# A two-layer spectral and gated network on one core: the 32-point transforms as 64x64 matrix cells, two frequency groups at a time

## The chip, the cores and the metric

The kernel runs on one core of a Trainium2 chip. The metric is device time in microseconds (us) of one execution; the median of several runs counts, and less is better. The engines are named as in the profile: PE multiplies matrices (PEld is its weight loading), DVE and ACT are the vector and the scalar engine, POOL is GpSimd, SP issues most DMAs. SBUF is the on-chip memory, PSUM the accumulator memory that PE writes, with eight banks of 128 partitions by 512 float32.

## What is computed

Two layers, each a global spectral filter and a bilinear gated block, on an input of 2048 rows by 512 features in float32:

```python
x = x + irfft2(rfft2(layernorm(x)) * (w_r + 1j * w_i))     # over rows (2048) and features (512)
h = layernorm(x)
x = x + ((h @ w_gate) * (h @ w_up)) @ w_down               # 512 -> 1792 -> 512
```

Both lines are executed twice, with the same weights in both layers.

## The kernel before

The rows are split as 2048 = 64 x 32. One spectral filter is three stages. The **forward stage** (`fwd`, `fwd_rest`, line 528 on) takes 16 row tiles `t`: it folds and transforms the 512 features, then multiplies by a twiddled 64-point matrix (`times`, tile `sp`, four products with 64 rows of the array each), and ACT copies the spectrum into `E`, with 256 feature frequencies and one edge frequency (index 256).

The **middle stage** (`middle`, line 606) does the 32-point transforms, the filter and the inverse 32-point transforms. Before the change it goes over 16 groups `n` of 16 frequencies, each a tile of 128 partitions (real and imaginary part, two row halves, 32 points) by 512 elements. For one group:

1. `turn(n, False)`: DVE transposes 32x32 blocks of `E` into `T`.
2. PE multiplies by the block matrix `f2` (128x128, with four copies of a 32-point matrix and zeros between) into the PSUM bank `zp`.
3. The complex product with the filter. Eleven groups of 16: ACT copies the two halves of `zp` crosswise with a change of sign into `jz` (two instructions of 64 partitions), DVE multiplies `zp` by the filter's real part, POOL multiplies `jz` by its imaginary part, and DVE adds the two into `ys`. Five groups (`PE_ADDS`: 2, 6, 8, 10, 14): ACT copies `zp` to `jz` with one instruction, DVE and POOL multiply as before, and PE does the addition by multiplying `ys` by `g2` and `jz` by `g2j` into the same bank.
4. PE multiplies by the inverse matrix `g2` into the bank `yp`, ACT copies it back to `T`, and `turn(n, True)` transposes it on DVE into `E`.

The edge frequency is done by a small product of 32 columns (`xp`, `tx`) whose result DVE adds to group 0; group 0's first frequency takes its filter from `hp` by separate small instructions.

The filter's pieces come by SP in eight loads of 1 MB (`wq`, `wr`); two of them, pieces 6 and 7, are loaded when pieces 0 and 1 are no longer wanted. In the same stretch of the first layer POOL and ACT also split the first weights of the gated block into high and low parts (`wt` from `rg`, `wd` and `u` from `rw`).

The **inverse stage** (`inv`, line 687) multiplies rows of `E` by twiddles (`vp`), transforms the features (`yi`), and adds to `xs`, the running value. Then `build_x` (line 757) lays the normalised rows out as high and low parts (`xA`, `xS`, with the help of `sx` or `sw`), and the gated block's products (`gx`, `gy`, `gz`, `gw`, `gv`, `db`, `ex` and the like) begin. They fill most of the time.

What sets the order: every piece of work is an operation of `Plan` with an engine, a price and a due time. `Plan.order` simulates the engines, the buffers and the DMA bus with these prices, and repeats this with 163 changes of due times drawn from the seeds in `MOVES`; the instructions are then issued in the order of the last simulation. Each engine works through its own instructions strictly in that order. Due times of the middle stage are 2.1 us a group, and the stage after it is due 36 us later (line 1099). Small float32 buffers such as `jz` and `ys` share the ring `f` of ten; the PSUM banks are the rings `x`, `y`, `w` (one each), `d` (two) and `a` (three).

Of the kernel before, what the change touches and what calls it, by code (L numbers as in the profile page):

```python
# [26 lines left out]
def consts():  # L27
# [32 lines left out]
    r[64:, :, 64:] = c  # L60
    c, s = _cs(j[:, None] * j[None], 32)
    z = np.zeros((32, 32))
    bd = lambda a: np.block([[a, z], [z, a]])
    f2 = np.block([[bd(c), bd(-s)], [bd(s), bd(c)]])
    g2 = np.block([[bd(c), bd(s)], [bd(-s), bd(c)]]) / 2048
    mid = np.concatenate([f2, g2, np.concatenate([g2[64:], -g2[:64]]), np.eye(128)], 1).astype(np.float32)
# [4 lines left out]
PE_ADDS = (2, 6, 8, 10, 14), (2, 6, 8, 10, 14)  # L71
POOL_ADDS = (), ()
# [13 lines left out]
MOVES = (  # L86
# [19 lines left out]
RATE = 270.0  # L106
WARM = 2
EARLY = 0
HOLD, FAR = {"DVE": 1.0, "ACT": 1.0, "POOL": 1.0}, 15.0
CLEAR = 1.5  # L110
FREE = ("a", "f", "st", "s1", "s2", "s3")
LOOK, SLACK = 0.08, 20.0
# [21 lines left out]


class Draw:


    def __init__(self, seed):
        self.at = seed * 0x9E3779B97F4A7C15 % 2 ** 64  # L140

    def part(self):
        self.at = (self.at + 0x9E3779B97F4A7C15) % 2 ** 64
        z = self.at
        z = (z ^ z >> 30) * 0xBF58476D1CE4E5B9 % 2 ** 64
        z = (z ^ z >> 27) * 0x94D049BB133111EB % 2 ** 64
        return ((z ^ z >> 31) >> 11) * 2.0 ** -53

    def one(self, of):
        return of[int(self.part() * len(of))]  # L150

    def bell(self):
        return (self.part() + self.part() + self.part() + self.part() - 2.0) * 1.7320508


class Plan:
# [38 lines left out]
    def order(self, hop=0.12):  # L195

        ops = self.ops
        for o in reversed(ops):
            d = min([ops[s]["due"] for s in o["suc"]] + [1e9 if o["due"] is None else o["due"]])
            o["due"] = d - 1.1 * o["lag"] - hop - 0.3 * (o["e"] == "PE")  # L200
        self.kinds = [(o["e"], *(t.name for t in o["tiles"])) for o in ops]
        out, marks = self.run([], [])
        for n in MOVES:
            out, marks = self.run(out, *self.move(n, out, marks)[:1])
        return out

    def move(self, n, out, marks):


        ops, draw = self.ops, Draw(n)  # L210
        end = max(o["end"] for o in out)
        lo, span = -20.0 + draw.part() * (end + 10.0), draw.one((10.0, 20.0, 40.0, 80.0, 160.0))
        share, jit, way = draw.one((0.0, 0.25, 0.5, 1.0)), draw.one((0.0, 0.0, 2.0, 5.0)), draw.part()
        inside = [o for o in ops if lo < o["start"] < lo + span]
        if way < 0.4 and inside:
            kind, by = self.kinds[draw.one(inside)["i"]], 8.0 * draw.bell()
            for o in inside:
                if self.kinds[o["i"]] == kind:
                    o["due"] += by
        elif way < 0.7 and inside:  # L220
            for _ in range(1 + int(3.0 * draw.part())):
                draw.one(inside)["due"] += 8.0 * draw.bell()
        elif inside:
            self.latest(out, end)
            shifts = sorted(o["late"] - o["due"] for o in inside)
            shift = shifts[len(shifts) // 2]
            for o in inside:
                o["due"] += share * (o["late"] - shift - o["due"]) + jit * draw.bell()
        return [m for m in marks if m[1] < lo - 15.0], lo + span

    def latest(self, out, end):
        ops = self.ops
        nxt, two = {}, None
        for o in reversed(out):
            long = o["end"] - o["start"]
            late = end - long
            for s in o["suc"]:
                late = min(late, ops[s]["late"] - (0.0 if ops[s]["next_to"] is o else long))
            if o["e"] in nxt:
                late = min(late, nxt[o["e"]] - o["pitch"])  # L240
            if o["two"]:
                if two is not None:
                    late = min(late, two - o["pitch"])
                two = late
            for t in o["tiles"]:
                if t in self.after:
                    late = min(late, self.after[t]["late"] - long)
            nxt[o["e"]] = late
            o["late"] = late

    def run(self, best, marks, pace=None, look=LOOK, hop=0.12, slack=SLACK):

        ops = self.ops
        marks = list(marks)
        m, rings, free, bus, port, after = 0, {}, {"SP": 0.75, "AQ": 0.75, "PE": 0.9, "POOL": 0.5}, 0.75, 0.0, {}
        if marks:
            m, _, rings, free, bus, port, after = marks[-1]
        rings, free, after, out = {g: list(q) for g, q in rings.items()}, dict(free), dict(after), best[:m]
        done, mark = sum(o["e"] == "PE" for o in out), marks[-1][1] if marks else 0.0
        ready, turn = {}, {}  # L260
        for o in ops:
            o["n"], o["out"] = len(o["pre"]), False
            for t in o["tiles"]:
                t.left, t.slot, t.freed, t.due = t.users, None, 0.0, None
        for o in out:
            o["out"] = True
            for s in o["suc"]:
                ops[s]["n"] -= 1
            for t in o["tiles"]:
                t.left -= 1  # L270
                t.slot, t.freed = True, max(t.freed, o["end"])
        for o in sorted(ops, key=lambda o: (o["due"], o["i"])):
            for t in o["tiles"]:
                if t.due is None:
                    t.due = o["due"]
                    if t.slot is None:
                        turn.setdefault(t.ring, []).append(t)

        def enter(o):
            o["at"] = max([ops[p]["start" if ops[p] is o["next_to"] else "end"] for p in o["pre"]], default=0.0)  # L280
            ready.setdefault(o["e"], []).append(o)

        for o in ops:
            if not o["n"] and not o["out"]:
                enter(o)
# [961 lines left out]
```

## Time and profile before

| | us |
|---|---|
| runs: lowest, median, highest of 3 | 1091.39, 1092.04, 1097.29 |
| profiled execution: span from its first to its last instruction (the profile gives no other time for it) | 1088.8 |
| PE busy | 1073.3 (99%) |
| DVE busy | 835.3 (77%) |
| POOL busy | 728.6 (67%) |
| ACT busy | 456.7 (42%) |
| first middle stage, from DVE's first transpose to the first full-rate product of the inverse stage | 48.84 to 85.73 |
| second middle stage, likewise | 590.96 to 626.90 |

The profile names work by the tile that it writes and the tiles that it reads, `out<-in`, with buffer numbers left out: `zp<-T,midt` is a product with the matrix `midt` into `zp`. All operations are recorded at one line, so names tell them apart. A float32 product appears as two MATMUL records. PE's busy time is modelled from its pipeline, so a busy PE need not be at its peak. In the chain of work that ended last, every piece is followed back to what released it.

### The profile page before, as it was taken

To read this page: it belongs to the slowest core of one execution; us is meant where nothing else is said; L and a number is where in the kernel's file an instruction comes from. 1 tells how busy PE (TensorE), PEld (TensorE's weight loads), DVE (VectorE), ACT (ScalarE), POOL (GpSimd) and SP (SyncE) were. 2 spreads that over 40 slices of the span, in tenths; PEclk is the share of its full clock that TensorE was granted. 3 is DMA by queue.
4 is the path that set the end of the run, shared out by engine and by line. 5 is a ranking of instruction groups with operands and counts; after the bars stand their busy time and mean duration, and the time that the engine had idled before them with its cause. 6 is when DMAs were issued, how large, how long until landed. Compare 5 with 4: busy or idle time off the path is not lost.

```text
span 1088.8 us, 18587 instructions
## 1 busy us (share of the span) xinstructions
PE 1073.3 (99%) x6484; PEld 923.3 (85%) x6484; DVE 835.3 (77%) x1684; ACT 456.7 (42%) x1045; POOL 728.6 (67%) x938
## 2 busy tenths in 40 slices
PE   8999999999999999999999999999999999999998
PEld 6748988888899988888996489888889998888887
DVE  8497957777878766776797978777888876667777
ACT  6787643334442223323347776133443521222230
POOL 6486799797988665556774627566556984666680
PEclk9999999999999999999999999999999999999999
DMA  8564256574652655555354313565545256555542
GB/s 316 190 224 158 86 204 243 201 260 152 236 203 76 208 184 200 169 180 170 112 198 151 135 54 101 204 196 168 175 151 192 70 193 223 190 181 188 197 146 78
DMA packets 50445, 189.56 MB, mean 174 GB/s; under 512 B 5296, under 2 KB 19248, under 8 KB 39344
## 3 DMA queue, kind: packets, MB, share of 16 engines
q0 software_dynamic: 16128, 102.77, 28.7%
q1 hardware_dynamic: 33792, 85.01, 22.1%
q8 instruction: 52, 0.85, 0.3%
q10 hardware_dynamic: 432, 0.59, 0.1%
q14 instruction: 41, 0.34, 0.1%
HBM read 145.62 MB, written 42.73 MB: 173 GB/s over the span
## 4 chain that ended last, share of the span: by engine, by line
PE 90%; DVE 6%; DMA 2%; ACT 1%; issue 1%; POOL 0%; SPq 0%; DVEq 0%; ACTq 0%
PE gz L389 14%; PE gx L389 14%; PE db L389 7%; PE gv L389 7%; PE gw L389 7%; PE gy L389 7%; PE ex L389 5%; PE ez L389 5%; PE yi L389 3%; PE sp L389 3%; PE ey L389 3%; PE ev L389 3%; PE ew L389 3%; PE dp L389 2%; PE vp L389 2%; PE zp L389 2%
## 5 line engine op out<-in xcount | busy, mean ns | idle before, releaser
L389 PE MATMUL gx<-xA,wt 128*128 128x512 f32 (+1 forms) x852 | 180.8, 347 | 1.4 <-DVE xA L389 1.1
L389 PEld LDWEIGHTS gx<-xA,wt 128*128 128x128 f32 x852 | 136.6, 190 | 18.6 <-DVE xA L389 1.5
L389 DVE TENSOR_TENSOR q<-gy,s 128x512 f32<-128x512 f32 (+1 forms) x71 | 41.1, 578 | 79.9 <-PE gy L389 75.0
L389 DVE TENSOR_TENSOR xs<-xs,db 128x512 f32<-128x512 f32 x128 | 86.3, 683 | 18.3 <-PE db L389 18.1
L389 POOL TENSOR_TENSOR sf<-cc,sf 128x256 fp32r<-128x256 f32 x101 | 74.3, 738 | 32.9 <-ACT sf L389 32.4
L389 ACT CAST sf<-q 128x256 fp32r<-128x256 f32 x90 | 36.7, 408 | 132.6 <-DVE q L389 76.8
L389 POOL DMA_DIRECT2D wt<-gu x72 | 40.2, 558 | 76.0 <-PE gz L389 57.5
L389 PE MATMUL gz<-xS,wt 128*128 128x512 f32 (+1 forms) x426 | 90.1, 347 | 0.7 <-DVE q L389 0.7
L389 PE MATMUL gw<-xS,wt 128*128 128x512 f32 (+1 forms) x426 | 90.4, 347 | 0.0
L389 PE MATMUL gv<-xS,wt 128*128 128x512 f32 (+1 forms) x426 | 90.2, 347 | 0.0
L389 PE MATMUL db<-wd,h 128*128 128x512 f32 x336 | 90.1, 394 | 0.0
L389 PE MATMUL gy<-xS,wt 128*128 128x512 f32 (+1 forms) x426 | 89.9, 346 | 0.0
L389 PE MATMUL gz<-xA,wt 128*128 128x512 f32 (+1 forms) x426 | 89.8, 346 | 0.0
L389 POOL TENSOR_TENSOR sf<-q,sf 128x256 fp32r<-128x256 f32 x90 | 66.5, 740 | 21.3 <-ACT sf L389 19.8
L389 PEld LDWEIGHTS gz<-xA,wt 128*128 128x128 f32 x426 | 69.6, 189 | 9.9
L389 PEld LDWEIGHTS gy<-xS,wt 128*128 128x128 f32 x426 | 68.9, 189 | 9.3 <-issue 0.3
L389 PEld LDWEIGHTS gz<-xS,wt 128*128 128x128 f32 x426 | 68.5, 190 | 9.7 <-DVE q L389 1.2
L389 PEld LDWEIGHTS gw<-xS,wt 128*128 128x128 f32 x426 | 68.3, 190 | 8.7 <-DVE gz L389 0.3
L389 PEld LDWEIGHTS gv<-xS,wt 128*128 128x128 f32 x426 | 68.1, 190 | 8.1
L389 ACT CAST sf<-cc 128x256 fp32r<-128x256 f32 x101 | 41.0, 406 | 76.8 <-PE ez L389 22.6
L389 ACT COPY s<-gx 128x512 f32<-128x512 f32 (+1 forms) x71 | 35.2, 496 | 86.8 <-PE gx L389 81.0
L389 POOL TENSOR_TENSOR wt<-rg,wt 128x512 fp32r<-128x512 f32 (+1 forms) x56 | 63.7, 1154 | 8.8 <-ACT wt L389 8.7
(169 smaller groups left out, 2667.2 us busy)
## 6 DMA issues: line engine op xcount, KB each, us to landing
wt<-gu POOLq DMA_DIRECT2D x36, 1024.0 KB, 5.3
wt<-gu POOLq DMA_DIRECT2D x36, 768.0 KB, 4.7
bf<-dn POOLq DMA_DIRECT2D x20, 1024.0 KB, 5.5
bf<-dn POOLq DMA_DIRECT2D x20, 768.0 KB, 4.7
gu<-wt SPq DMA_DIRECT2D x14, 1024.0 KB, 6.6
gu<-wt SPq DMA_DIRECT2D x14, 768.0 KB, 3.5
wq<-in_wf_dram SPq DMA_DIRECT2D x10, 1024.0 KB, 6.2
rg<-in_wb_dram SPq DMA_DIRECT2D x14, 512.0 KB, 4.6
```

The source lines that it names most:

```text
L389: ins = f(*args, **kw)
```

## The change

It touches the middle stage, its constants and the order of the whole program.

The matrices shrink to 64x64 (real and imaginary part by 32 points) and stand twice, on partitions 0 to 63 and 64 to 127. Rows of the constants of the forward and the inverse stage are permuted so that a partition half holds one row half `b` (real and imaginary). The loop goes over eight pairs `m` of frequency groups. Its forward product is four cells, one for each of two groups `par` and two row halves `b`; the cell reads partitions of half `b`, and writes partitions of half `par` in bank `zp[b]`. After it a partition half is one group instead of one row half:

```diff
-            pe(0.86, lambda z=z, n=n: TE.matmul(z(), f2, T()[:, 16 * n:16 * n + 16], start=True, stop=True), [(T, n), "midt"], [zp])
+            zp = [bank("zp", tag) for tag in ("xy", "dd")[i % 2]]
+            def spec(zp=zp, m=m):
+                for par, b in ((0, 0), (1, 1), (1, 0), (0, 1)):
+                    n = 2 * m + par
+                    cell(k3(zp[b], half[par]), f2[b], T()[half[b], 16 * n:16 * n + 16], True, True)
+            pe(0.88, spec, [(T, 2 * m), (T, 2 * m + 1), "midt"], zp)
```

All additions of the complex product go to PE: for each bank one full copy by ACT, one product by the real part, one by the imaginary part, and two accumulated rounds of four cells, with `g2` and with `g2j`:

```diff
+            for b in range(2):
+                alone = (m, b) in ON_DVE_MID
+                if not alone:
+                    act(512, lambda b=b, q=q, zp=zp: A.copy(q[b](), k3(zp[b])), [zp[b]], [q[b]])
+                if (m, b) in on_pool:
+                    pool(512, lambda b=b, q=q, y=y, m=m: gtt(y[b](), q[b](), W(m, 0, b), ALU.mult), [q[b], W.key(m, 0)], [y[b]])
+                else:
+                    dve(512, lambda b=b, y=y, zp=zp, m=m: tt(y[b](), k3(zp[b]), W(m, 0, b), ALU.mult), [zp[b], W.key(m, 0)], [y[b]])
+                if alone:
+                    dve(512, lambda b=b, q=q, zp=zp, m=m: tt(q[b](), k3(zp[b]), W(m, 1, b), ALU.mult), [zp[b], W.key(m, 1)], [q[b]])
+                else:
+                    pool(512, lambda b=b, q=q, m=m: gtt(q[b](), q[b](), W(m, 1, b), ALU.mult), [q[b], W.key(m, 1)], [q[b]])
+            yp = [bank("yp", tag) for tag in ("aa", "aw")[i % 2]]
+            cells = (0, 0), (1, 1), (0, 1), (1, 0)
+            def unspec(g, z, edge, start, yp=yp, m=m):
+                for par, b in cells:
+                    cell(k3(yp[par], half[b]), g[par], z[b]()[half[par]], start, not start and m + par > 0)
+                for b in range(2 * (m == 0)):
+                    cell(yp[0]()[half[b], 0:32], g[0], ty[:, edge, b], False, not start)
+            for g, z, edge in ((g2, y, 0), (g2j, q, 1)):
+                pe(0.88 + 0.08 * (m == 0), lambda g=g, z=z, edge=edge, f=unspec: f(g, z, edge, edge == 0),
+                   [*z, *([("ty", edge, b) for b in range(2)] if m == 0 else []), *(yp if edge else ())], yp)
```

with `ON_POOL_MID = ((3, 0), (5, 0))` and `ON_DVE_MID = ((7, 0), (7, 1))`. The transposes (`turn`, two at each end of a pair) and ACT's copies of `yp` to `T` stay, 32 and 16 of them in a stage. Group 0's first frequency is written into the filter's own buffers once (`W.edge`, two small ACT copies), and the edge frequency takes one small transpose, two small cells, four small DVE products (`ty`) and two small cells in each round of pair 0. Loads have the same sizes as before, but for the matrix (96 KB and 64 KB in place of 192 KB and 64 KB).

The order of the whole program is no longer simulated: `ORDER` is a written-out list of all 4987 operations, and `Plan.order` reads it. The due times behind it have 3.3 us a pair in the middle stage and 29 us from it to the next (`MID`, in place of 36).

More of the change, by code (lines that the diff above doesn't have):

```diff
@@ L193, in op @@
         return o
[L195 to L244, printed above, removed]
-            for t in o["tiles"]:
[L246 to L285, printed above, removed]
-        while len(out) < len(ops):
-            nexts = []
-            for e, cand in sorted(ready.items(), key=lambda r: free.get(r[0], 0.0)):
-                if nexts and free.get(e, 0.0) > min(a for a, _ in nexts) + look:
-                    break
-                can = []
-                for o in cand:
-                    at = max(o["at"], free.get(e, 0.0), port if o["two"] else 0.0)
-                    if e == "SP":
-                        at = max(at, o["due"] - o["ahead"])
-                    want, early = {}, False
-                    for t in o["tiles"]:
-                        if t.slot is None:
-                            early = early or t.due > turn[t.ring][0].due + (slack if t.ring in self.FREE else 0.0)
-                            want[t.ring] = want.get(t.ring, 0) + 1
-                    if early:
-                        continue
-                    for g, n in want.items():
-                        when = sorted(t.freed for t in rings.get(g, ()) if not t.left)
-                        n -= self.RINGS.get(g, 1) - len(rings.get(g, ()))
-                        at = max(at, 1e9 if n > len(when) else when[n - 1] if n > 0 else 0.0)
-                    if at < 1e9:
-                        can.append((at, o))
-                if can:
-                    first = min(a for a, _ in can)
-                    take = min(((a, o) for a, o in can if a <= first + look), key=lambda c: (c[1]["due"], c[1]["i"]))
-                    if e in HOLD:
-                        soon = [(a, o) for a, o in can if a < take[0] + HOLD[e] * take[1]["pitch"] and o["due"] < take[1]["due"] - FAR]
-                        take = min(soon, key=lambda c: (c[1]["due"], c[1]["i"]), default=take)
-                    nexts.append(take)
-            if not nexts:
-                raise AssertionError([(o["e"], o["i"], [t.ring for t in o["tiles"]]) for c in ready.values() for o in c][:40])
-            first = min(a for a, _ in nexts)
-            if first > mark + 20.0:
-                mark = first
-                marks.append((len(out), first, {g: list(q) for g, q in rings.items()}, dict(free), bus, port, dict(after)))
-            at, o = min((c for c in nexts if c[0] <= first + look), key=lambda c: (c[1]["due"], c[1]["i"]))
-            if o["e"] == "PE":
-                assert not pace or at < pace[done]
-                done += 1
-            ready[o["e"]].remove(o)
-            for t in o["tiles"]:
-                if t.slot is None:
-                    t.slot = True
@@ L330, in run, with order @@
+    def order(self):
+        ops = [self.ops[int(ORDER[i:i + 3], 36)] for i in range(0, len(ORDER), 3)]
+        rings, done = {}, set()
+        for n, o in enumerate(ops):
+            assert o["pre"] <= done
+            done.add(o["i"])
+            for t in o["tiles"]:
+                if not t.users:
+                    continue
+                if t.left == 0:
+                    t.left = t.users
                     q = rings.setdefault(t.ring, [])
@@ L332, in run @@
                     if len(q) == self.RINGS.get(t.ring, 1):
-                        old = min((u for u in q if not u.left), key=lambda u: u.freed)
-                        after[old] = o
+                        old = min((u for u in q if not u.users), key=lambda u: u.freed)
                         q.remove(old)
@@ L337, in run @@
                     q.append(t)
-                    turn[t.ring].remove(t)
-            o["start"] = at
-            free[o["e"]] = at + o["pitch"]
-            if o["two"]:
-                port = at + o["pitch"]
-            if o["kb"]:
-                bus = max(bus, at) + o["kb"] / RATE
-                o["end"] = max(at + o["lag"], bus + 2.3)
-            else:
-                o["end"] = at + o["lag"] + hop + 0.3 * (o["e"] == "PE")
+                t.freed = n
             for t in o["tiles"]:
                 t.left -= 1
-                t.freed = max(t.freed, o["end"])
-            out.append(o)
-            for s in o["suc"]:
-                ops[s]["n"] -= 1
-                if not ops[s]["n"]:
-                    enter(ops[s])
-        self.after, self.marks = after, marks
-        return out, marks
+                if not t.left:
+                    t.users = 0
+        assert len(done) == len(self.ops)
+        return ops
 @with_exitstack
@@ L430 @@
     pe(0.86, lambda: TE.matmul(wp()[:, 0:256], warm()[:, 0:128], warm()[:, 0:256], start=True, stop=True), [warm], [(wp, 9)], due=5.5)
-    midt = cp.tile([128, 512], F32, name="midt")
-    f2, g2, g2j, ident = (midt[:, 128 * i:128 * i + 128] for i in range(4))
+    midt = cp.tile([128, 320], F32, name="midt")
+    f2, g2, g2j = ([midt[64 * r:64 * r + 64, 64 * i:64 * i + 64] for r in range(2)] for i in range(3))
+    ident = midt[:, 192:320]
     def aq(kb, fn, w, due, lag):
@@ L597, in load, with key, __call__, edge @@
             load(1024, lambda: SP.dma_start(self.at[n][2](), wf[:, n // 2, n % 2]), (), [self.at[n][0]])
-        def key(self, n, i):
-            return self.at[2 * (n // 4) + i][0]
-        def __call__(self, n, i, lo=0):
-            kw = 16 * (n % 4)
-            return self.at[2 * (n // 4) + i][2]()[:, kw + lo:kw + 16]
-    def middle(E, W, t0, adds):
+        def key(self, m, i):
+            return self.at[2 * (m // 2) + i][0]
+        def __call__(self, m, i, b):
+            at = 32 * (m % 2) + 16 * b
+            return self.at[2 * (m // 2) + i][2]()[:, at:at + 16]
+        def edge(self):
+            for i in range(2):
+                act(64, lambda i=i: A.copy(self.at[i][2]()[0:64, 0:32:16], hp[:, i, 0].rearrange("p (b g) -> p b g", b=2)),
+                    ["hp"], [self.at[i][0]])
+    def middle(E, W, t0, on_pool):
         T = temp("T", "xS", (128, 256, 32))
+        first = [(E, t, j) for t in range(15) for j in range(2)]
         def turn(n, back, due=None):
@@ L610, in turn @@
             t = lambda: T()[:, 16 * n:16 * n + 16].rearrange("p k (t j) -> p k t j", j=2)
-            es = [(E, t_, j) for t_ in range(15) for j in range(2)] + [(E, 15, j, n > 3) for j in range(2)]
             if back:
@@ L614, in turn @@
             else:
-                dve(512, lambda: V.transpose(t(), e()), es, [(T, n), (E, "b", n)], due=due)
-        def times_w(z, jz, w, p):
-            return ((lambda: A.mul(jz()[0:64], z()[64:128], -1.0)), (lambda: A.copy(jz()[64:128], z()[0:64])),
-                    (lambda: tt(p(), z(), w(0), ALU.mult)), (lambda: gtt(jz(), jz(), w(1), ALU.mult)))
-        order = [1, 2, 3, 0, *range(4, 16)]
-        for i in range(16):
-            n = order[i]
-            if n == 8:
+                dve(512, lambda: V.transpose(t(), e()), first + [(E, 15, j, n > 3) for j in range(2)], [(T, n), (E, "b", n)], due=due)
@@ new lines, in cell, with last_bin, spec @@
+        def cell(o, w, z, start, stop):
+            TE.matmul(o, w, z, start=start, stop=stop, skip_group_check=True)
+        k3 = lambda o, rows=slice(0, 128): o()[rows].rearrange("p (k g) -> p k g", g=32)
+        half = [slice(0, 64), slice(64, 128)]
+        def last_bin(due):
+            dve(100, lambda: V.transpose(tx.rearrange("p (t j) -> p t j", j=2), E()[:, :, 256]),
+                first + [(E, 15, j, True) for j in range(2)], ["tx"], due=due)
+            xp = [bank("xp", "aw"[b]) for b in range(2)]
+            def spec():
+                for b in range(2):
+                    cell(xp[b]()[0:64, 0:32], f2[b], tx[half[b]], True, True)
+            pe(0.15, spec, ["tx", "midt"], xp)
+            for b in range(2):
+                dve(40, lambda b=b: tt(ty[:, 0, b], xp[b]()[0:64, 0:32], hp[:, 0, 1, 32 * b:32 * b + 32], ALU.mult),
+                    [xp[b], "hp"], [("ty", 0, b)])
+                dve(40, lambda b=b: tt(ty[:, 1, b], xp[b]()[0:64, 0:32], hp[:, 1, 1, 32 * b:32 * b + 32], ALU.mult),
+                    [xp[b], "hp"], [("ty", 1, b)])
@@ L642, in middle @@
-            zp = bank("zp", "xydwd"[i % 5])
-            z = lambda zp=zp: zp().rearrange("p (k g) -> p k g", g=32)
-            pe(0.86, lambda z=z, n=n: TE.matmul(z(), f2, T()[:, 16 * n:16 * n + 16], start=True, stop=True), [(T, n), "midt"], [zp])
-            q = temp("jz", "f", (128, 16, 32))
-            y = temp("ys", "f", (128, 16, 32))
-            where = adds[n]
-            fs = times_w(z, q, lambda i, n=n: W(n, i), y if where != "DVE" else z)
-            if where == "PE":
-                act(512, lambda z=z, q=q: A.copy(q(), z()), [zp], [(q, 0), (q, 1)])
-            else:
-                act(512, fs[0], [zp], [(q, 0)], more=0.11)
-                act(512, fs[1], [zp], [(q, 1)], more=0.11)
@@ L674, in middle @@
-            yp = bank("yp", "a")
-            ms = [y, q] if where == "PE" else [y]
-            def unspec(yp=yp, ms=ms):
-                y3 = yp().rearrange("p (k g) -> p k g", g=32)
-                for j, m in enumerate(ms):
-                    TE.matmul(y3, g2j if j else g2, m(), start=j == 0, stop=j == len(ms) - 1)
-            pe(0.86 * len(ms), unspec, [y, (q, 0), (q, 1)], [yp])
-            act(512, lambda yp=yp, n=n: A.copy(T()[:, 16 * n:16 * n + 16], yp().rearrange("p (k g) -> p k g", g=32)),
-                [yp], [(T, n)], more=0.07)
@@ L685, in middle @@
-            turn(n, True, due)
+            due = t0 + 8 + MSTEP * i
+            for par in range(2):
+                turn(2 * m + par, False)
+            if m == 0:
+                last_bin(due)
+            zp = [bank("zp", tag) for tag in ("xy", "dd")[i % 2]]
[3 more added lines that the diff above has]
+                    cell(k3(zp[b], half[par]), f2[b], T()[half[b], 16 * n:16 * n + 16], True, True)
@@ new lines, in middle @@
+            pe(0.88, spec, [(T, 2 * m), (T, 2 * m + 1), "midt"], zp)
+            q = [temp("jz", "f", (128, 16, 32)) for _ in range(2)]
+            y = [temp("ys", "f", (128, 16, 32)) for _ in range(2)]
+            for b in range(2):
+                alone = (m, b) in ON_DVE_MID
[9 more added lines that the diff above has]
+                    pool(512, lambda b=b, q=q, m=m: gtt(q[b](), q[b](), W(m, 1, b), ALU.mult), [q[b], W.key(m, 1)], [q[b]])
@@ L687, in inv @@
+            for par in range(2):
+                n = 2 * m + par
+                act(512, lambda yp=yp, n=n, par=par: A.copy(T()[:, 16 * n:16 * n + 16], k3(yp[par])), [yp[par]], [(T, n)], more=0.07)
+                turn(n, True, due)
     def inv(t, nm, E, di, mode, tags, due=None, on_act=False, early=None):
@@ L1075, in down @@
         add(gz, R[1], 0, at(7) + 0.7)
-    ADDS = [{n: "PE" if n in PE_ADDS[i] else "POOL" if n in POOL_ADDS[i] else "DVE" for n in range(16)} for i in range(2)]
     dcs = {}
@@ L1097 @@
         W.load(3)
[L1098 to L1099 removed]
+        middle(E, W, t0, ON_POOL_MID)
+        t0 += MID
         X = temp("xA", "xA", (128, 3, 2, 2, 512), F32R), temp("xS", "xS", (128, 4, 2, 2, 512), F32R)
```

239 lines of the change are left out of this document (169 added, 70 removed), and 19 rows, old and new, of the table MOVES.

## The prediction

> **What bounds the kernel now.** I read the page first.
>
> ```profile
> span 1088.8 us, 18587 instructions
> PE 1073.3 (99%) x6484; PEld 923.3 (85%) x6484; DVE 835.3 (77%) x1684; ACT 456.7 (42%) x1045; POOL 728.6 (67%) x938
> DVE  8497957777878766776797978777888876667777
> PE 90%; DVE 6%; DMA 2%; ACT 1%; issue 1%; POOL 0%; SPq 0%; DVEq 0%; ACTq 0%
> ```
>
> Over the whole span PE is the bound. But DVE's slices have 9s in two places, and 6% of the chain is DVE. A table of windows, cut at the two middle stages, shows whose stages these are (columns: length, then busy time of PE, PEld, DVE, ACT and POOL, clock, DMA share, GB/s):
>
> ```profile
> 0.00:48.80 48.80, 45.53 (x326) 35.34 (x326) 29.39 (x105) 34.13 (x87) 26.55 (x40) 1.00 0.66 235
> 48.80:85.70 36.90, 34.71 (x88) 15.42 (x88) 36.80 (x64) 29.09 (x55) 30.92 (x29) 1.00 0.60 227
> 85.70:103.80 18.10, 18.06 (x118) 16.77 (x119) 12.38 (x40) 14.12 (x36) 8.45 (x12) 1.00 0.57 200
> 103.80:590.90 487.10, 484.42 (x2948) 426.00 (x2946) 365.41 (x734) 193.57 (x443) 357.36 (x439) 1.00 0.53 181
> 590.90:626.90 36.00, 34.22 (x89) 15.61 (x89) 35.85 (x64) 25.54 (x48) 20.86 (x19) 1.00 0.36 124
> 626.90:1075.00 448.10, 447.06 (x2872) 406.87 (x2873) 345.51 (x659) 159.05 (x378) 283.41 (x400) 1.00 0.48 160
> 1075.00:1088.80 13.80, 9.27 (x48) 7.31 (x46) 9.96 (x19) 1.22 (x3) 1.02 (x2) 1.00 0.41 153
> ```
>
> In the second and fifth row DVE is busy 36.80 of 36.90 us and 35.85 of 36.00. The stage cannot be shorter than DVE's list of work. PE is busy some 34 us beside it, so DVE's list alone could give 2 us at most; the change cuts PE's work there too, which is costed below. The chain has the same ends (start, length, what):
>
> ```profile
> 48.84 0.72 DVE T L389
> 80.91 4.78 DVE E L389 x8
> 85.73 2.64 PE vp L389 x20
> ...
> 590.96 0.72 DVE T L389
> 622.67 4.19 DVE E L389 x7
> 626.90 1.70 PE vp L389 x12
> ```
>
> Each stage starts with DVE's first transpose and ends when its last one lets the inverse stage's `vp` go. So what leaves DVE's list shortens the span, until another engine or the filling and draining of the pipeline takes over.
>
> **The change, part by part. DVE.** The groups of DVE's instructions in the first stage (the second has the same counts):
>
> ```profile
> L389 DVE STREAM_TRANSPOSE T<-E 128x512 f32<-128x512 f32 x16 | 10.3, 680 | 6.0 <-ACT E L389 6.0
> L389 DVE STREAM_TRANSPOSE E<-T 128x512 f32<-128x512 f32 x16 | 10.3, 679 | 0.0
> L389 DVE TENSOR_TENSOR ys<-zp,jz 128x512 f32<-128x512 f32 x11 | 7.3, 660 | 0.0
> L389 DVE TENSOR_TENSOR zp<-zp,wq 128x512 f32<-128x512 f32 (+1 forms) x9 | 5.9, 673 | 0.0
> L389 DVE TENSOR_TENSOR ys<-zp,wq 128x512 f32<-128x512 f32 x3 | 2.0, 668 | 0.0
> L389 DVE TENSOR_TENSOR ys<-ys,tx 128x32 f32<-128x32 f32 x1 | 1.2, 1155 | 0.0
> L389 DVE TENSOR_TENSOR zp<-zp,hp 128x32 f32<-128x32 f32 x1 | 0.2, 199 | 0.0
> ```
>
> Two more rows hold four products with `wr`. That makes 32 transposes, 16 products and 11 additions, 59 large instructions. One lasts 0.67 us, but they overlap: seven transposes in 4.19 us are 0.599 each, and 59 x 0.599 = 35.3 of the 36.9 us. Small ones fill the rest; `ys<-ys,tx` alone is 1.2 us.
>
> Afterwards there are 32 transposes, 14 products with the real part (two of 16 go to POOL) and two with the imaginary part (`ON_DVE_MID`): 48 x 0.599 = 28.8 us. The 11 additions are gone. The small ones become one transpose and four products, costed at 0.1 us apart (the 0.2 us of `zp<-zp,hp` overlaps as the large ones do): 0.5 us. Sum 29.3 us of DVE work in each stage.
>
> To it comes time that DVE cannot fill. At the start it has 16 transposes to go on with. At the end the last pair's second round (0.86 us, below) and ACT's copy must pass before its transpose:
>
> ```profile
> 625.23 0.58 ACT L389 COPY T<-yp 128x512 f32<-128x512 f32 x1 [0.27 <-PE yp L389]
> ```
>
> 0.86 + 0.27 + 0.58 is 1.7, with the steps between engines some 1.8 us if no other transpose is left, and nothing if three are held back, as the seven and eight in a row above are now. I take 0.5, near the lower end since transposes are held back now, and keep 0 to 1.8. So 29.8 us (29.3 to 31.1).
>
> **PE.** Whether it stays below this depends on the cells. Nothing in the trace has 64x64 cells; the nearest rows are products on half the array's rows, beside full ones:
>
> ```profile
> 45.59 2.87 PE L389 MATMUL sp<-us,tw 64*128 64x257 f32 x24
> 45.58 2.47 PEld L389 LDWEIGHTS sp<-us,tw 64*128 64x128 f32 x24
> 49.61 4.56 PE L389 MATMUL zp<-T,midt 128*128 128x512 f32 x10 [1.16 <-DVE T L389]
> 69.63 1.88 PE L389 MATMUL zp<-T,midt 128*128 128x512 f32 x4
> ...
> L389 PEld LDWEIGHTS zp<-T,midt 128*128 128x128 f32 x64 | 11.6, 189 | 18.9 <-issue 10.0 <-DVE T L389 6.8 <-DVE ys L389 0.8
> ```
>
> A full product of 512 columns is two records, 0.86 us apart from the next (four records in 1.88, their last one ending 0.16 late; ten in 4.56). The run of `sp` is three times four products of 256 columns, which by that pace would take 3 x 1.72 = 5.2 us one after another; it took 2.87. So products on the two row halves do run at once, and two of 512 columns cost 0.95 where the ideal is 0.86. Loads of their weights come every 0.10 us (2.47/24), so they too overlap.
>
> If all four cells of a round run at once, a round costs 0.86, or 0.95 with the loss of `sp`. There are three rounds a pair, 24 a stage: 20.6 to 22.8 us, below DVE's 29.3. If only the row halves overlap, a round is two such steps, 1.72 to 1.90. I take the lower, because cells on different column halves have as little in common as cells on different row halves, and keep the higher for a rival.
>
> The full-height rows say something of weight loading: ten records with ten loads of 0.19 us between them stand 0.43 apart, so the loads are hidden behind products on the same rows. [...]
>
> **POOL and ACT.** POOL multiplies 14 imaginary parts and two real ones, 16 large instructions as now; two small ones go.
>
> ```profile
> L389 POOL TENSOR_TENSOR jz<-jz,wr 128x512 f32<-128x512 f32 x8 | 10.1, 1269 | 2.8 <-ACT jz L389 2.8
> L389 POOL TENSOR_TENSOR wt<-rg,wt 128x512 fp32r<-128x512 f32 (+1 forms) x5 | 5.8, 1164 | 2.6 <-ACT wt L389 2.6
> 103.78 1.54 POOL L389 TENSOR_TENSOR sx<-sx 128x256 f32<-128x256 f32 x2 [7.82 <-ACT sx L389]
> ```
>
> 16 x 1.27 = 20.3 us is below 29.3. In the first stage POOL has weights to split besides, and its 30.92 us would fill a stage of 29.8. That work need not end there: after it POOL waits 7.8 us for `sx`, just before 103.8. A stage shorter by 7.1 uses that wait up almost wholly; with the idle inside the stage it still fits. The second stage has 20.86 us of POOL work, no such limit. ACT loses the crosswise halves: 14 copies and 16 to `T` at 0.58 are 17.4 us, where it is busy 25 to 29 now. DMA sizes are the same, and pieces 6 and 7 of the filter are asked for after the same groups, so they come no later against the loop.
>
> **The rest of the program** gets another order. In the windows outside the middle stages, start and end, PE is idle 0.04 + 2.68 + 1.04 = 3.8 us, so a better order has under 4 us to win there and some 3 at the start (48.80 less 45.53). A worse one can lose; the nearest row is POOL's 7.8 us wait, one stall of that length. With no reason for a sign I take 0.
>
> **The sum.** First stage 36.9 - 29.8 = 7.1 us, second 36.0 - 29.8 = 6.2 us, together 13.3. The span goes from 1088.8 to 1075.5. The median of the runs, 1092.0, lies 3.2 above the span (start and end outside it), which I carry over: 1078.7, so **1079 us**. With the bounds of the tail the same sum is 1077.7 to 1081.3.
>
> **The rivals.**
>
> *Row halves only (slower).* Two cells on the same rows but different columns do not run at once. Then a stage is PE's: 24 rounds of 1.72 to 1.90 are 41.3 to 45.6 us, with 1.2 us of transposes ahead and 2.1 behind (ACT's copy and two transposes) 44.6 to 48.9; two stages lose 16 to 25 us: 1108 to 1117. It decides from a round of 29.3/24 = 1.22 us on. [...] Against it: row halves do run so, and the loads hide.
>
> *POOL takes DVE's place in the first stage.* If its weight work stays ahead of the products, or the products come in bunches, `sx` is late. At worst the first stage's 7.1 us are lost: 1086; half of it gives 1082. For it: 30.92 us of work in a stage of 29.8. Against it: its wait of 7.8.
>
> *The order is better or worse elsewhere.* Better by the 4 to 7 us of idle PE time: 1072 to 1075. Worse by one stall of 7.8: 1087.
>
> **How the numbers follow.** Forecast 0.56 (own range 1076 to 1083), POOL in the first stage 0.14 (1082 to 1086), better order 0.12 (1071 to 1076), worse order 0.09 (1083 to 1092, split evenly at the bound below), row halves only 0.09. About 0.5%, or 5.5 us, is what a measurement of this kernel can tell from no change: faster is below 1086.5. So faster is 0.56 + 0.14 + 0.12 + 0.04 = 0.86, the same 0.05, slower 0.09. The range takes the forecast, POOL and most of both orders: 1071 to 1087.
>
> **What would show it.** In the profile after: middle stages of some 30 us, with DVE busy nearly throughout and no `ys<-zp,jz` rows; 48 large DVE instructions in each; PE busy some 21 to 25 us in them, and each round of eight `zp` or `yp` records within 0.86 to 0.95 us; ACT's busy time in both down by some 14 us together; POOL's wait for `sx` nearly gone. Rounds of 1.7 us or more, with DVE idle for `zp` or `yp`, would show the slower rival. A first middle stage of 30 us followed by a longer way to the first `gx` would show POOL's. A stage above 32 us with DVE idle inside would mean that filling and draining cost more than 1.8, which makes this sum wrong.

## The result, and the profile after

The median after is 1077.56 us (1076.85 to 1077.94, 4 runs) against 1091.72 us before (1089.9 to 1097.29, 4 runs). The ratio is 0.9858, with a 95% interval of 0.9828 to 0.9887: 1.4% faster. The profiled execution took 1076.85 us, with a span of 1075.1, so 1.75 us lie outside the span.

From the page of the kernel after:

```profile
span 1075.1 us, 19053 instructions
PE 1056.2 (98%) x6740; PEld 917.3 (85%) x6740; DVE 823.0 (77%) x1662; ACT 438.4 (41%) x1019; POOL 730.6 (68%) x934
PE 92%; DVE 5%; ACT 1%; issue 1%; POOL 0%; DMA 0%; DVEq 0%; POOLq 0%; ACTq 0%
```

The windows of the kernel after, cut at its own middle stages (columns as in the prediction's table):

```profile
49.34:79.66 30.32, 26.74 (x221) 14.07 (x221) 29.35 (x53) 18.86 (x38) 24.71 (x23) 0.94 0.53 196
79.66:97.20 17.54, 16.59 (x108) 15.34 (x109) 11.14 (x38) 13.94 (x35) 15.77 (x18) 1.00 0.68 241
97.20:584.28 487.08, 484.70 (x2954) 427.02 (x2952) 367.74 (x738) 194.73 (x449) 358.96 (x440) 1.00 0.54 184
584.28:613.75 29.47, 26.73 (x216) 11.31 (x217) 29.35 (x53) 16.25 (x32) 20.39 (x17) 1.00 0.43 151
```

The first row and the last are the two stages, 30.32 and 29.47 us, with DVE busy 29.35 us in both. Before they were 36.89 (48.84 to 85.73) and 35.94 (590.96 to 626.90). So 6.57 + 6.47 = 13.04 of the 13.7 us between the spans come out of these two stages; the remaining 0.7 us is the sum of small differences elsewhere (0.5 longer ahead of the first stage, 0.6 shorter between the stages and 0.6 behind the second). In the clock column, the first row's 0.94 is new; below it gets a part of its own.

The chain of the kernel after has the stages' ends where they were, at DVE's first transpose and at its last (the x8 and x7 rows are the transposes in a row that end a stage):

```profile
74.84 4.78 DVE E L353 x8
79.66 2.18 PE vp L353 x16
...
584.28 0.72 DVE T L353
609.52 4.19 DVE E L353 x7
613.75 1.70 PE vp L353 x12
```

DVE's groups of the kernel after in the second stage:

```profile
L353 DVE STREAM_TRANSPOSE T<-E 128x512 f32<-128x512 f32 x16 | 10.3, 679 | 5.9 <-ACT E L353 5.9
L353 DVE STREAM_TRANSPOSE E<-T 128x512 f32<-128x512 f32 x16 | 10.2, 683 | 0.0
L353 DVE TENSOR_TENSOR ys<-zp,wq 128x512 f32<-128x512 f32 x11 | 7.1, 662 | 0.1
L353 DVE TENSOR_TENSOR ys<-zp,wr 128x512 f32<-128x512 f32 x3 | 1.9, 673 | 0.0
L353 DVE TENSOR_TENSOR jz<-zp,wq 128x512 f32<-128x512 f32 x2 | 1.3, 666 | 0.0
L353 DVE TENSOR_TENSOR ty<-xp,hp 64x32 f32<-64x32 f32 x4 | 0.5, 168 | 0.0
```

48 large instructions, no `ys<-zp,jz`. And PE's rounds of four cells, from the timeline of PE of the kernel after (start, length with the tail of the last record, what):

```profile
595.81 1.09 PE L353 MATMUL zp<-T,midt 64*64 64x512 f32 x8
596.72 1.04 PE L353 MATMUL yp<-jz,midt 64*64 64x512 f32 x8
597.57 1.04 PE L353 MATMUL yp<-ys,midt 64*64 64x512 f32 x8
598.43 1.44 PE L353 MATMUL zp<-T,midt 64*64 64x512 f32 x6
```

The second, third and fourth start 0.85 and 0.86 us apart: four cells of 512 columns take as long as one product on the full array (0.86 us in the kernel before).

### The profile page after: what moved, and what is told of

Same layout as the page of the kernel before. It is cut to its first block, busy times and chain, and to the rows that moved or that the text cites. A ratio compares the mean times of both kernels' runs of the same rounds, so it can differ in the third digit from the quotient of the medians.

```text
span 1075.1 us, 19053 instructions
## 1 busy us (share of the span) xinstructions
PE 1056.2 (98%) x6740; PEld 917.3 (85%) x6740; DVE 823.0 (77%) x1662; ACT 438.4 (41%) x1019; POOL 730.6 (68%) x934
## 4 chain that ended last, share of the span: by engine, by line
PE 92%; DVE 5%; ACT 1%; issue 1%; POOL 0%; DMA 0%; DVEq 0%; POOLq 0%; ACTq 0%
PE gz L353 15%; PE gx L353 15%; PE db L353 8%; PE gv L353 7%; PE gy L353 7%; PE gw L353 7%; PE ez L353 5%; PE ex L353 5%; PE yi L353 3%; PE ev L353 3%; PE ey L353 3%; PE ew L353 3%; PE vp L353 2%; PE sp L353 2%; PE dp L353 2%; PE tq L353 1%
## 5 line engine op out<-in xcount | busy, mean ns | idle before, releaser
L353 POOL TENSOR_TENSOR sf<-q,sf 128x256 fp32r<-128x256 f32 x96 | 71.2, 742 | 50.9 <-ACT sf L353 48.9
L353 POOL TENSOR_TENSOR sf<-cc,sf 128x256 fp32r<-128x256 f32 x98 | 72.6, 742 | 30.3 <-ACT sf L353 29.7
L353 POOL DMA_DIRECT2D wt<-gu x72 | 40.4, 561 | 69.5 <-PE gz L353 41.9
L353 ACT CAST sf<-q 128x256 fp32r<-128x256 f32 x96 | 39.1, 407 | 106.4 <-DVE q L353 42.4
L353 PEld LDWEIGHTS db<-wd,h 128*128 128x128 f32 x336 | 60.8, 189 | 10.9
```

The lines of the kernel that those rows point to most:

```text
L353: ins = f(*args, **kw)
```

## The experiments

Stage lengths below run from DVE's first transpose of the stage to the end of its last (after: 30.27 and 29.42; before: 36.84 and 35.89). All experiments change the kernel after, but for two that change the one before. Runs without a range are single executions with a profile.

**DVE's list made as long as before.**

```diff
-                    dve(512, lambda ...: tt(y[b](), k3(zp[b]), W(m, 0, b), ALU.mult), [zp[b], W.key(m, 0)], [y[b]])
+                    def real(b=b, y=y, zp=zp, m=m):
+                        for _ in range(1 + ((m, b) not in ((0, 0), (1, 0), (2, 0)))):
+                            tt(y[b](), k3(zp[b]), W(m, 0, b), ALU.mult)
+                    dve(512, real, [zp[b], W.key(m, 0)], [y[b]])
```

> In each middle stage DVE does 11 of its 14 products with the filter's real part twice, with the same operands and target; PE, POOL, ACT and the order of the program are those of the change. Theory (the stage lasts as long as DVE's list): 11 x 0.599 = 6.6 us more in each stage, so stages of about 36.9 and 36.1 us in place of 30.3 and 29.5, and 13 us on the whole, near 1090. First rival (the time came from PE's shorter work): PE's work is unchanged, so stages within 1 us of 30.3 and 29.5 and a time near 1078. Second rival (the time came from the new order of the program outside these stages): the stages grow, but then they must have been longer with the change than without, which the trace excludes; it expects no particular number.

1095.81 us. Windows of its two stages, and of the time around and behind the end of the second:

```profile
49.45:86.72 37.27, 30.41 (x220) 12.02 (x220) 36.87 (x64) 18.85 (x38) 26.95 (x24) 0.95 0.43 161
592.95:630.27 37.32, 31.50 (x212) 11.58 (x213) 36.87 (x64) 16.25 (x32) 20.50 (x17) 0.97 0.35 119
626.00:632.00 6.00, 4.55 (x24) 3.67 (x25) 4.26 (x8) 1.07 (x2) 0.00 (x0) 0.65 0.01 3
```

DVE is busy 36.87 of 37.27 and 37.32 us: the stages follow its list, by 7.0 and 7.9 us where 6.6 was expected, and the first rival falls. The second had been excluded by the windows above, which leave 0.7 us outside the stages. The time rose by 18 us, 5 more than expected; the span, on which the windows lie, by 18.9. 1.7 us more than expected are in the stages, 1.6 between them, and 2.3 behind the second. In the third row PE ran at 0.65 of its clock around the stage's end. At a clock of 0.50 from 630.27 to 632.00, with PE busy throughout, it lost some 0.9 us of the 2.3 behind the stage (an estimate: half of 1.73 us). What the clock was behind 632.00 the row does not show, so the rest of the 2.3 us is not explained, nor are the 1.6 us between the stages.

**More work for PE, in front of DVE's products.**

```diff
-                for par, b in ((0, 0), (1, 1), (1, 0), (0, 1)):
+                for par, b in 2 * ((0, 0), (1, 1), (1, 0), (0, 1)):
```

> In each middle stage every round of forward cells is issued twice, eight rounds more of 0.86 us each, 6.9 us of PE work; nothing else changes. Theory (DVE's list sets the stage): PE's work grows from 20.7 to 27.6 us and stays under DVE's 29.3, so each stage grows by 0 to 2 us, from waits of single pairs; time 1078 to 1082. Rival (PE's work sets it): each stage grows by 6.9 us, time near 1091.

1085.22 us, stages of 35.05 and 33.42 us:

```profile
48.83:83.88 35.05, 31.39 (x284) 18.69 (x284) 29.73 (x53) 19.34 (x38) 27.34 (x25) 1.00 0.47 171
588.57:621.99 33.42, 31.18 (x280) 19.19 (x280) 29.95 (x53) 16.25 (x32) 20.55 (x17) 1.00 0.37 133
```

Neither expectation: they grow by 4.8 and 4.0 us, where the theory had at most 2 and the rival 6.9. DVE now idles 5.3 and 3.5 us. So PE had far less reserve than its rounds suggest. The timelines show where it was. In the second stage of the change PE works from 585.13 to 610.67 with no wait above 0.27 us, 25.5 us for rounds that sum to 20.6 (the edge frequency's small cells aside), and the stage ends 3.0 us later. With eight rounds more it works from 589.43 to 619.27, and the stage ends 2.7 us later. So 6.9 us of added work made PE's stretch 4.3 us longer, and DVE's last transposes hide 0.3 of it. Two further runs ask what kind of reserve this is.

**Half as much, and the same amount behind DVE's products.** The first edit doubles the forward round in every second pair, the second doubles the first inverse round:

```diff
-                for par, b in ((0, 0), (1, 1), (1, 0), (0, 1)):
+                for par, b in (1 + m % 2) * ((0, 0), (1, 1), (1, 0), (0, 1)):
```

```diff
-                for par, b in cells:
+                for par, b in (1 + start) * cells:
```

> The round of forward cells is issued twice in every second pair only, four rounds (3.4 us of PE work) more a stage. With eight more the stages grew by 4.8 and 4.0 us, where the theory that DVE's list sets the stage had 0 to 2. If PE had a fixed reserve that eight rounds used up (6.9 less 4.8 and less 4.0, so 2.1 to 2.9 us), four cost 0.5 to 1.3 us a stage, time 1078.5 to 1080. If every round added in front of DVE's products lengthens the path of its pair, four cost half of what eight do, 2.0 to 2.4 us a stage, time near 1082.

> The first inverse round of each pair (the one with the products by the real part) is issued twice, also eight rounds more, but behind DVE's products and not in front of them; pair 0's two small edge cells go twice too. If PE's amount of work is what counts, the stages grow as with eight more forward rounds, by 4 to 5 us, time near 1085. If it is the wait of DVE for its products' input, they grow by under 2 us, time 1078 to 1081.

Four more rounds: 1082.59 us, stages of 33.24 and 31.99, longer by 3.0 and 2.6. Eight more behind: 1085.36 us, stages of 34.84 and 33.43, longer by 4.6 and 4.0, as with eight in front. So it is PE's amount of work that counts, not on which side of DVE's products it is, and there is no fixed reserve that must be used up first: each added round of 0.86 us costs 0.50 to 0.60 us where eight are added, and 0.64 to 0.74 where four are. Whether an order made anew for the longer rounds would hide them was not tried.

**Cells on the same rows next to each other.**

```diff
-                for par, b in ((0, 0), (1, 1), (1, 0), (0, 1)):
+                for par, b in ((0, 0), (1, 0), (0, 1), (1, 1)):
...
-            cells = (0, 0), (1, 1), (0, 1), (1, 0)
+            cells = (0, 0), (0, 1), (1, 0), (1, 1)
```

> In every round the two cells on the same half of the array's rows are issued one right after the other, where the change alternates the row halves; the products are the same. If the four cells of a round run at once whatever their order, a round stays at 0.86 us and the time within 2 us of 1077.6. If products (or loads of weights) on the same rows wait for each other, rounds grow: only the middle two of four cells then overlap, so a round is up to three steps in place of two, 1.3 us or more, PE's work in a stage 31 us or more, and the time 1081 to 1095.

1076.55 us, stages of 29.89 and 29.35. The timeline of PE:

```profile
596.31 1.04 PE L353 MATMUL yp<-jz,midt 64*64 64x512 f32 x8
597.16 1.04 PE L353 MATMUL yp<-ys,midt 64*64 64x512 f32 x8
598.02 1.43 PE L353 MATMUL zp<-T,midt 64*64 64x512 f32 x8
```

0.85 and 0.86 us apart again. Cells that share rows run at once and their weight loads are hidden, in both orders: four cells with their eight loads take 0.85 to 0.86 us in each. The rival of waiting on the same rows falls.

**The additions on PE, without the cells.** Both edits are to the kernel before; the first is the basis for the second. (`MOVES` has 167 entries, not the 163 named above.)

```diff
-MOVES = (
-    1400000003, ...)
+MOVES = ()
```

```diff
-PE_ADDS = (2, 6, 8, 10, 14), (2, 6, 8, 10, 14)
+PE_ADDS = tuple(range(1, 16)), tuple(range(1, 16))
```

> The kernel before with MOVES empty: its order is that of the first simulation, without the 163 later changes of due times. It is the basis for the next two, which use the same simulation. Middle stages of 36 to 38 us; elsewhere the order is worse, by an unknown amount: 1092 to 1115.

> As the run without moves, but with the additions of 15 of the 16 groups of each middle stage on PE, as products of the full 128x128 matrices: the change's shift of work from DVE to PE without its cells. DVE's list falls to 49 large instructions, 29.4 us, but PE has 47 products of 0.86 us, 40.4 us. Theory (a stage lasts as long as the longest list, and the cells are what makes room on PE): stages of 41 to 45 us, 10 to 16 us slower than the run without moves. Rival (DVE's list alone counts): stages of about 30 us, 13 us faster.

1113.6 us without moves, with stages of 38.33 and 37.72; 1123.18 us with 15 additions on PE as full products, 9.6 slower, with stages of 43.43 and 42.96:

```profile
51.19:94.62 43.43, 42.24 (x108) 19.58 (x108) 31.44 (x54) 22.84 (x43) 32.75 (x32) 1.00 0.50 184
608.29:651.25 42.96, 42.19 (x108) 19.58 (x108) 31.53 (x54) 20.04 (x37) 20.92 (x19) 1.00 0.31 109
```

DVE's list is nearly as short as the change makes it (busy 31.4 and 31.5 us, 29.35 with the change), and the stage is longer: PE is busy 42.2 us of it. The 47 full products of 0.86 us are 40.4 us in any order, more than either stage of the kernel before. So the additions can leave DVE only because the cells make room on PE.

**The change with the simulated order.** The list `ORDER` goes, and `Plan.order` with its simulation comes back from the kernel before, with `MOVES = ()`.

> The change with its operations ordered by the simulation of the kernel before, without moves, in place of the written-out list. Theory (the stages give the whole gain, the list next to nothing outside them): against the run without moves both stages are shorter by 5 to 7 us each and the whole by 10 to 14. Rival (much of the gain is the list's): the difference is under 6 us, while the written-out list stands 13 us below.

1106.46 us, stages of 33.36 and 34.98:

```profile
51.75:85.11 33.36, 28.93 (x216) 11.61 (x216) 29.74 (x52) 18.13 (x35) 26.94 (x24) 1.00 0.55 208
599.24:634.22 34.98, 30.55 (x216) 12.64 (x216) 29.75 (x52) 15.93 (x30) 20.39 (x17) 0.95 0.38 129
```

Against 1113.6 that is 7.1 us, between the two expectations. DVE has the same list of 29.7 us, but stands idle 3.6 and 5.2 us of the stages, mostly since its products come before their inputs (some 4 of the 5.2 us are in front of `ys`). So under one and the same simulation the change gives about half of what it gave, and the written-out order is what lets DVE's list become the stage's length. What the moves in the kernel before were worth in these stages is 1.5 and 1.8 us; the list is worth 3.1 and 5.6 to the change. Up to 1.7 of the 5.6 us may be the clock's (an estimate: the mean of 0.95 over 34.98 us). The list alone, without the change, could not have shortened the stages of the kernel before: DVE is busy 36.80 of 36.84 us and 35.85 of 35.89 there, so no order makes room while its work stays the same.

**The first pair's transposes first.** In the first stage of the kernel after PE waited long, and then ran slowly. Timeline of PE, and a window behind the wait:

```profile
51.97 3.59 PE L353 MATMUL zp<-T,midt 64*64 64x512 f32 x16 [2.92 <-DVE T L353]
52.50:55.00 2.50, 2.50 (x16) 0.83 (x10) 1.58 (x4) 1.00 (x2) 0.29 (x1) 0.50 0.91 365
```

Two rounds take 3.59 us, where the same two take 1.95 us in `dve_eleven_more` (the run with 11 products more) at a clock of 1.00: here the granted clock is 0.50. The order has DVE transpose groups 3, 4, 1, 2, 0, 5 while PE begins with groups 2 and 3. The edit puts six places of the list right:

```diff
+        turns = list(self.turns.values())[0]
+        at = {o["i"]: n for n, o in enumerate(ops)}
+        for n, k in zip(sorted(at[turns[k]] for k in range(16))[:6], (3, 2, 1, 0, 4, 5)):
+            ops[n] = self.ops[turns[k]]
```

> In the first middle stage of the change DVE's transposes begin with groups 3, 4, 1, 2, 0, 5, while PE begins with the pair of groups 2 and 3: it sat idle for 2.9 us, and its granted clock was 0.50 for the next 3.4 us. Here the first six are 3, 2, 1, 0, 4, 5; all else is unchanged. Theory (the idle time brought the lower clock, as in no other stage): PE waits some 1.3 us as in the second stage, the clock stays at 1.00, DVE's idle time of 0.9 us in this stage goes, and the stage shrinks from 30.3 by 0.5 to 0.9 us; time 1076.7 to 1077.1. Rival (the lower clock comes from the 64x64 cells themselves or from the heavy DMA traffic at that time, with or without the idle time): the clock is again 0.50 for some us, and the stage stays within 0.3 us.

1076.96 us (1076.0 to 1078.34, 4 runs), stages of 29.24 and 29.42:

```profile
50.98 2.18 PE L358 MATMUL zp<-T,midt 64*64 64x512 f32 x16 [1.74 <-DVE T L358]
49.52:78.76 29.24, 25.96 (x220) 13.69 (x220) 29.23 (x53) 19.11 (x38) 25.03 (x23) 1.00 0.55 205
```

The wait is 1.74 us where 1.3 was expected, the clock stays at 1.00, and the stage is exactly DVE's list, 29.23 of 29.24 us, 1.0 us shorter. The rival falls: the cells are the same and DMA is as busy (a share of 0.99 in the window from 52.5 to 55.0). In the time of the whole it cannot be told from the scatter of the runs.

**Less for DVE, more for POOL, in the second stage.** On top of the edit above, with operations put off in the list until their inputs are there:

```diff
-        middle(E, W, t0, ON_POOL_MID)
+        middle(E, W, t0, ON_POOL_MID + (((0, 0), (2, 0), (6, 0)) if layer else ()))
```

> The change with the first pair's transposes first, and in the second middle stage three more products with the real part on POOL ((0,0), (2,0), (6,0) besides (3,0), (5,0)); operations whose inputs then come too late are put off until these are there. DVE's list in that stage falls by 3 x 0.599 = 1.8 us to 27.5, POOL's grows by 3 x 1.27 = 3.8 to 24.2. Theory (DVE's list sets the stage): the second stage falls from 29.5 to some 28 us, time near 1075.5. Rival (POOL's longer chain for a pair, two or three products of 1.27 us one after another before PE's second round, now ends last): the stage stays at 29.5 or grows by 1 to 3 us.

1078.7 us (1077.98 to 1079.17, 5 runs); the second stage is 31.89 us, 2.5 longer, with DVE busy 28.16. Its chain ends:

```profile
609.44 1.23 POOL jz L370
610.67 0.04 issue
610.72 1.14 PE yp L370 x7
611.86 0.57 ACT T L370
612.43 0.02 issue
612.46 3.10 DVE E L370 x5
```

The rival's number holds, and at the end its reason too: POOL's last product now lets PE's last round go, and DVE's last transposes wait for that. But DVE stands idle 3.7 us in all: 1.8 in front of transposes, and 1.9 in front of products, which wait for ACT's copies and once for POOL. What POOL's longer chain and what the operations put off cost of these was not taken apart. A shorter list for DVE is worth nothing if the paths of the pairs grow.

**Both harmless edits together, beside the change on one chip.** First pair first, and cells on the same rows next to each other:

> The first pair's transposes first, and the cells on the same rows next to each other, together; each alone took the first middle stage from 30.3 to 29.2 and 29.9 us. Theory: a stage cannot go below DVE's list of 29.2 us, so the stages are 29.2 and 29.4 us, as with the first edit alone, and the time is 1076.5 to 1077, within 1 us of the change. If the two add up, the first stage is 28.9 us.

> The change itself once more, beside the run with both edits on the same chip: 1077 to 1078, with the granted clock below 1.00 in the first middle stage's first microseconds.

1076.22 us (1074.98 to 1077.74, 4 runs) and 1076.24 us (1075.48 to 1077.04, 5 runs); stages of 29.18 and 29.34 against 29.96 and 29.42. The first stage is 0.8 us shorter in the profile, and the medians are the same (the change alone came out a little below the 1077 to 1078 that were expected). No version was found that is measurably faster than the change.

## Why the prediction was right

It said 1079 (1071 to 1087), and 1077.56 was measured. Point by point:

- **The stages are set by DVE's list, which loses 11 additions.** Right: 29.3 us of work was forecast, 29.35 is in both windows. Lengthening the list by 11 products made the stages as long as before and 0.4 and 1.4 us longer.
- **Time that DVE cannot fill, 0.5 us a stage.** The size was near, the place wrong. At the end nothing is lost: eight and seven transposes were held back. The second stage has 0.1 us of idle time. The first has 0.9, in the middle of its start, where PE ran at a granted clock of 0.50; the prediction had no such step. So 7.1 + 6.2 was forecast and 6.57 + 6.47 came. That it stayed below the upper bound of 1.8 hangs on the written-out list: with the simulated order DVE's idle time is 3.6 and 5.2 us. The prediction had no row for that, so this term was in part luck.
- **A round of four cells takes 0.86 us.** Right, with both orders of the cells. The traces of both orders show 0.85 to 0.86 us a round, so a round is one step and not two.
- **PE stays below DVE.** Right for the change, but the reserve was overrated. PE is busy 26.7 us in each stage where 21 to 25 were named, as the cells of a round do not all start together: in the second stage the first one starts at 585.13, behind DVE's first transpose (584.28 and 0.72 long), where its pair needs two. Added rounds cost time even when only four are added. The rival of row halves only was worked out as if PE's rounds simply summed, so its point of decision would lie below 1.22 us a round; where, no run shows.
- **POOL in the first stage.** Right that it fits. Its wait for `sx`, 7.82 us before, is now 1.48, since more of the weights are split behind the stage; from POOL's timeline after:

```profile
99.34 1.54 POOL L353 TENSOR_TENSOR sx<-sx 128x256 f32<-128x256 f32 x2 [1.48 <-ACT sx L353]
```

- **The order elsewhere, 0.** Right: 0.7 us. But the order within the stages is not neutral: with one simulation for both kernels the whole change gives 7.1 us, not 14.2.
- **ACT's copies.** Both stages together lost 19.5 us of ACT's busy time, where 14 were named. ACT sets nothing here, so the sum does not depend on it.
- **What lies outside the span, 3.2 us.** Mis-sized. It is 1.75 us after, and 1.76 in a later run of the kernel before (1090.26 with a span of 1088.5). The 3.2 set the median against the span of one of the faster executions. With 1.75 in its place the same sum gives 1077.3.

## What to carry to other kernels

Where one engine is busy for a stage's whole length, count its instructions there at their spacing (0.60 us, not the 0.67 of one record), and the stage after can be read off before it is built. What is taken from it must fit the next engine (here the full products did not, the cells did), and the order must be made for it, or half is lost to waits. A sum that leaves another engine free time does not mean that more work for it costs nothing: here each added round cost more than half of its length.

## What the runs showed of the hardware that was not expected

PE's clock fell to half at the end of a wait of 2.92 us at the first stage's start: in the kernel after it is 1.00 up to 51.92 and 0.50 from there to 55.33. Seven runs here have this wait; in five of them the window from 52.5 to 55.0 shows a clock of 0.50 to 0.66, in two (`dve_eleven_more` and `pe_eight_more`, the runs with 11 products more and with eight rounds more in front) it shows 1.00. With a wait of 1.74 us it is 1.00 in all three runs, and so it is after the 1.16 us of the kernel before. But the length of one wait does not decide it: the clock also fell to half in `dve_eleven_more` behind a wait of 1.89 us, and again at its second stage's end, where the waits are 1.21 and 1.30 us long. In `after_no_moves` (the change with the simulated order) the second stage has a mean clock of 0.95, and behind a wait of 1.71 us single records of `zp` take 1.06 us where others take 0.59.

Windows ahead of a fall of the clock and behind it (the second column is PE's busy time), two of the kernel after and four of `dve_eleven_more`:

```profile
48.51:51.92 3.41, 0.54 (x5) 0.14 (x1) 2.58 (x5) 1.05 (x5) 0.00 (x0) 1.00 0.99 394
51.92:55.33 3.41, 3.36 (x16) 1.16 (x18) 2.49 (x6) 1.07 (x2) 0.62 (x1) 0.50 0.89 353
74.88:78.29 3.41, 1.52 (x12) 0.20 (x4) 3.31 (x7) 3.11 (x7) 3.41 (x4) 1.00 0.00 0
78.29:81.71 3.42, 3.42 (x17) 1.03 (x20) 3.38 (x6) 0.00 (x0) 3.18 (x5) 0.50 0.01 2
624.43:627.85 3.42, 1.59 (x14) 0.21 (x8) 3.42 (x7) 0.55 (x2) 0.00 (x0) 1.00 0.01 2
627.85:631.26 3.41, 2.72 (x12) 2.72 (x13) 2.41 (x5) 0.53 (x2) 0.00 (x0) 0.50 0.00 0
```

PE stood idle for part of each window ahead, with 0.54, 1.52 and 1.59 us of work in them. What decides that the clock falls was not shown; no run was made to test it.

Loads of 64x64 weights take 0.13 us in the records (`zp`, median 133 ns) where those of 128x128 took 0.19. Eight of them are 1.06 us, and a round with them takes 0.86 us, so they are hidden.
